# Two attention blocks on one core: layout changes through DRAM scratch, with a new planning table

## The chip, the cores and the metric

The kernel runs on one core of a Trainium2 chip. The metric is the device time of one execution in microseconds (us). A core has TensorE (PE, with its weight loads as PEld), VectorE (DVE), ScalarE (ACT), GpSimd (POOL) and SyncE (SP); in this kernel nearly all transfers are issued from SP's queue, one after the other.

## The reference

The input x is 1 x 2048 x 640. Two attention blocks with 32 heads of 20 read the same x, and a gate mixes them.

```python
x = A_x
g = sigmoid((x * gate_w).sum(-1, keepdims=True))
a = A(x, A_wqkv, A_wo)     # full softmax attention over 2048 keys
b = B(x, B_wqkv, B_wo)     # each query sees 8 keys: itself and 2, 4 .. 14 back, masked before the start
return g * a + (1 - g) * b
# A: scores = einsum("bhqd,bhkd->bhqk", q, k) * Dh**-0.5; softmax; einsum("bhqk,bhkd->bhqd"); @ wo
# B: logits over W=8 shifted copies of k (dil=2), softmax over the 8, weighted sum of 8 shifted copies of v; @ wo
```

## The kernel before, in words

**Block A.** Queries go in four chunks (`qc`) of 512 columns, heads in quads of four, so there are 32 groups `g`. A group has 64 units: 16 key blocks of 128 times 4 heads. A unit is a 128 x 512 tile of scores. TensorE writes the scores of 2 or 3 units into one of two score buffers (L1600), ACT takes the exponential of all of them in one instruction into `ebuf` (L1624), and TensorE multiplies by V into `obank` (L1669).

**The exponential on DVE.** Some units skip ACT: their scores "ride" along in a spare bank, and DVE writes an integer form of the exponential into `uD` (L1614). Four such units are a quad (`gen_d`): DVE adds three shifted copies `eD` (L863), POOL scales V (`vS`, L855), and TensorE sums four weighted products. The more quads, the less ACT has to do, and the more DVE and TensorE.

**Q's bounds.** `gen_qd` projects Q in slices of 128 features. A slice goes to `dst`, and a DMA for each piece of a head moves it into the rows of `qT` (L730). A matmul (L750) gives an upper bound of the scores for each head and query, which lies in `qbnd` with 32 heads times 4 column parts on the partitions (L757). It must become one row of 512 in `qT` for each head: for each run of heads of one quad, four DMAs (L770), one per column part.

**Block B.** It runs in 8 units `u` of 256 tokens. `gen_bproj` projects q, k and v into `qkvB` (v's part is called `vB`), with a halo of 16 tokens that POOL copies (L896). `vB` holds 4 groups of 32 heads on the partitions. Its shifted copies go to `vR`, part of the `kvw` tensor, so that each of four partition groups `w4` has all heads at its own shift: 16 DMAs per unit (L917). `gen_b` multiplies q with shifted k (L935), sums on TensorE, finds the maximum, takes the exponential `eB` on ACT (L983), and multiplies `eB` with `vR` (L1032). The reciprocal of the sum, with the gate in it, is `rQ` (L1013, L1015): 4 column parts on the partitions. Four DMAs bring it to 32 partitions of `rB` (L1018), and three more copy these to the other groups (L1020, `spread`). `rB` scales B's result into `oB` (L1065).

**Output.** `gen_norm` transposes and normalises A's result and moves it to `oTd` by DMAs for each piece (L841). `gen_fold` projects A and B for the first three query chunks; `gen_prefold` and `gen_prefold2` do this for the last chunk, as far as they can before the last group ends, and `tail` adds the last quad of heads (L1148 to L1175).

**The order.** All instructions are put in order when the kernel is built. `_Sched.task` keeps a planned clock for each engine, with a cost for each task: for a DMA, the time to its landing, and `iss` (0.75 us unless given) for each issue on SP. Each engine then runs its list in the fixed order, with semaphore waits. Side work (`gen_qd`, `gen_bproj`, `gen_b`, `gen_fold` and so on) are Python generators; each yields a request, for instance `("pe", cost, ready)`, and `run_side` takes the first one that fits into the gap that the exponentials leave. `wanted` decides whether a unit rides, and opens a quad only if enough time of the current groups remains (`DTIME`) and DVE is planned to be idle enough (`DIDLE`, `DIDLE2`, `DWAIT`). `PLAN` is the layout table: from score tile number `s` on, it sets 18 such parameters:

```python
(SLACK, XTOL, XPRIO, XLATE, DWAIT, DIDLE, DIDLE2, DTIME, DLOW, DLATE, DVE_AHEAD, DAHEAD, BOOST, XBOOST, RFILL,
 FILL, HOLD, BOFF) = plan
```

Of the kernel before, what the change touches and what calls it, by code (L numbers as in the profile page):

```python
# [5 lines left out]
FP32 = mybir.dt.float32  # L6
# [8 lines left out]
P = 128  # L15
# [35 lines left out]
    0: ((0.29, 0.69), 0.16, 1.0, 5.5, 0.94, -1.37, 0.17, 9.99, 5.5, 6.98, 0.6, 0.62, 5.69, 5.04, 0.0, 0.62, 2, -1.5),  # L51
    5: ((0.29, 0.69), 0.01, 1.0, 6.6, 1.12, -1.6, 0.17, 11.8, 2.0, 7.54, 0.6, 0.62, 4.85, 4.42, 0.0, 0.65, 2, -3),
    15: ((0.32, 0.64), 0.16, 1.0, 2.5, 0.94, -1.41, -0.97, 11.8, 7.0, 8.62, 0.62, 0.47, 4.4, 4.29, 0.0, 0.54, 2, -3),
    20: ((0.29, 0.69), 0.16, 1.0, 2.5, 0.94, -1.41, -0.97, 11.8, 7.0, 8.62, 0.62, 0.62, 5.69, 5.04, 0.0, 0.54, 2, -3),
    30: ((0.3, 0.63), 0.25, 1.0, 2.5, 1.39, -1.06, -0.43, 7.4, 7.0, 8.84, 0.7, 0.51, 4.4, 4.81, -0.2, 0.69, 1, -3),
    35: ((0.32, 0.68), 0.31, 2.5, 5.5, 0.76, -1.58, -0.5, 11.8, 7.0, 6.64, 0.35, 0.39, 4.4, 4.35, 0.0, 0.66, 2, -3),
    40: ((0.34, 0.69), 0.01, 1.0, 5.5, 0.94, -1.37, 0.17, 9.99, 7.0, 7.54, 0.6, 0.62, 5.69, 5.04, 0.0, 0.65, 2, -3),
    45: ((0.26, 0.66), 0.39, 1.0, 2.5, 0.49, -1.34, -0.97, 7.4, 7.0, 8.25, 0.52, 0.47, 4.4, 4.0, 0.0, 0.71, 3, 0.0),
    50: ((0.26, 0.75), 0.39, 1.0, 2.5, 0.49, -1.34, -0.97, 7.4, 7.0, 8.25, 0.52, 0.47, 4.4, 4.0, 0.0, 0.71, 3, 0.0),
    60: ((0.26, 0.75), 0.39, 1.0, 2.5, 0.49, -1.34, -0.97, 6.5, 7.0, 8.25, 0.43, 0.47, 4.4, 4.0, 0.0, 0.71, 3, 0),  # L60
    70: ((0.26, 0.75), 0.39, 1.0, 2.5, 0.81, -1.34, -0.97, 6.5, 7.0, 8.25, 0.43, 0.47, 4.4, 4.0, 0.0, 0.71, 0, 0),
    75: ((0.25, 0.75), 0.39, 1.0, 2.5, 0.81, -1.34, -0.97, 6.61, 7.0, 8.25, 0.43, 0.47, 4.4, 4.0, 0.0, 0.71, 0, 0),
# [12 lines left out]
    155: ((0.23, 0.7), 0.16, 1.0, 2.5, 0.94, -1.37, 0.49, 7.4, 5.5, 7.54, 0.45, 0.67, 5.69, 5.04, 0.0, 0.54, 1, -3),
    180: ((0.23, 0.7), 0.16, 1.0, 2.5, 0.94, -1.37, 0.49, 7.4, 5.5, 7.54, 0.45, 0.67, 5.69, 5.04, 0.0, 0.54, 1, 1),
    185: ((0.23, 0.7), 0.16, 5.5, 2.5, 0.94, -1.37, 0.49, 7.4, 5.5, 7.54, 0.45, 0.67, 5.69, 5.04, 0.0, 0.54, 1, -3),
    190: ((0.23, 0.7), 0.28, 5.5, 1.0, 0.94, -1.6, -0.5, 7.4, 5.5, 7.54, 0.52, 0.67, 4.64, 5.04, 0.0, 0.54, 1, -1.5),
    200: ((0.32, 0.64), 0.35, 5.5, 1.0, 0.94, -1.6, -0.5, 11.8, 7.0, 7.54, 0.52, 0.67, 4.4, 5.04, 0.0, 0.54, 1, -1.5),
    210: ((0.33, 0.64), 0.35, 5.5, 1.0, 1.02, -1.6, -0.5, 11.8, 7.0, 7.54, 0.52, 0.67, 4.4, 5.04, 0.0, 0.54, 1, -1.5),  # L80
    215: ((0.31, 0.76), 0.28, 2.5, 1.0, 0.72, -1.6, -0.65, 9.86, 7.0, 7.05, 0.52, 0.55, 5.68, 3.17, 0.0, 0.64, 2, -6),
    220: ((0.34, 0.68), 0.38, 2.5, 1.0, 0.94, -1.06, 0.05, 7.4, 7.0, 10.69, 0.6, 0.55, 3.3, 5.42, 0.0, 0.61, 1, -1.5),
    225: ((0.34, 0.68), 0.38, 2.5, 1.0, 0.82, -1.06, -0.35, 9.79, 7.0, 10.69, 0.61, 0.44, 4.4, 5.42, 0.0, 0.61, 1, 1),
    245: ((0.34, 0.68), 0.38, 2.5, 1.0, 0.82, -1.06, -0.35, 6.21, 7.0, 10.69, 0.61, 0.44, 4.4, 5.42, 0.0, 0.53, 1, 1),
    250: ((0.44, 0.72), 0.28, 2.5, 1.0, 1.21, -1.6, -0.5, 9.86, 7.0, 6.01, 0.45, 0.54, 6.04, 3.66, 0.0, 0.87, 0, -6),
    255: ((0.34, 0.68), 0.38, 2.5, 1.0, 0.94, -1.06, 0.05, 7.4, 7.0, 10.69, 0.6, 0.55, 3.3, 5.42, 0.0, 0.61, 1, -1.5),
# [293 lines left out]
def _build(ctx, nc, A_x, A_wqkv, A_wo, B_wqkv, B_wo, gate_w, out):  # L380
# [1482 lines left out]
```

## Time and profile before

| What | us |
|---|---|
| median of 3 runs (lowest, highest) | 810.18 (809.9, 811.21) |
| the profiled execution, and its span | 810.18, 808.3 |
| ACT: exponentials L1624, 707 instructions | 767.2 busy |
| DVE: L1614 (376 instructions), L863 (282) | 247.3 and 200.2 busy |
| DVE: B's products L935 and L1032, 40 each | 48.6 and 47.9 busy |
| PE: scores L1600, 2048 matmuls | 278.5 busy |

The span is the time from the first to the last instruction; 1.9 us lie around it. Busy time of an engine is the time in which at least one of its instructions ran, so the times of groups that overlap in the pipeline can't be added exactly. Lines such as L917 are lines of the kernel before. SPq is SP's queue: its rows show how long the issue of a DMA took, not how long the data moved.

### The profile page before, as it was taken

The page shows a single profiled execution, that of the slowest core. Times are in us where ns is not written, and L with a number is a line of the kernel's source. Part 1 is how long each engine was busy: PE and PEld are TensorE (multiplying, and loading weights), DVE is VectorE, ACT ScalarE, POOL GpSimd, SP SyncE. Part 2 cuts the span into 40 slices and gives each one's busy share as a digit, 9 for nine tenths or more (in the row PEclk, how much of TensorE's full clock was granted, in tenths as well). Part 3 has the DMA queues.
Part 4 walks back from the last instruction along what each step waited for, and adds up shares of the span by engine and source line. Part 5 has one row for each costly group of instructions (what it writes and reads, how often), then busy time and mean ns, then how long its engine had stood idle before and what let it go on. Part 6 is the DMA issues. An engine that isn't in the chain of part 4 may idle for free.

```text
span 808.3 us, 28593 instructions
## 1 busy us (share of the span) xinstructions
PE 749.0 (93%) x12063; PEld 285.9 (35%) x12065; DVE 721.9 (89%) x1236; ACT 779.0 (96%) x739; POOL 129.3 (16%) x193
## 2 busy tenths in 40 slices
PE   8999999999899898999999898999899899999987
PEld 5432222333233332333334323432334343234323
DVE  7587996589999999999999999899999999998865
ACT  4999999999999999999999999999999999999994
POOL 6011011011121110212112111121111212111010
PEclk9999999999999999999999999999999999999999
DMA  9112112300013131110013101313010310300221
GB/s 310 45 28 44 43 29 47 76 13 20 5 39 73 34 69 34 21 25 6 22 37 70 24 18 30 77 22 68 7 39 26 71 23 18 74 7 23 51 55 37
DMA packets 61458, 35.50 MB, mean 44 GB/s; under 512 B 27220, under 2 KB 60132, under 8 KB 61332
## 3 DMA queue, kind: packets, MB, share of 16 engines
q1 hardware_dynamic: 61044, 33.36, 17.0%
q8 instruction: 96, 1.57, 0.8%
q10 hardware_dynamic: 288, 0.33, 0.1%
q14 instruction: 30, 0.25, 0.1%
HBM read 12.00 MB, written 2.62 MB: 18 GB/s over the span
## 4 chain that ended last, share of the span: by engine, by line
PE 34%; DVE 32%; ACT 20%; issue 11%; SPq 1%; DMA 1%; POOL 0%; DVEq 0%; ACTq 0%; POOLq 0%
ACT ebuf L1624 20%; DVE uD L1614 12%; PE score L1600 10%; DVE eD L863 9%; PE side L623 9%; PE obank L1669 9%; PE score L623 3%; DVE kvw L935 3%; DVE kvw L1032 2%; DVE qkvB L909 2%; SPq L917 1%; PE obank L1690 1%; PE score L1315 1%; PE obank L523 1%; PE side L1042 1%
## 5 line engine op out<-in xcount | busy, mean ns | idle before, releaser
L1624 ACT ACTIVATE ebuf<-score 128x1024 bf16<-128x1024 f32 (+1 forms) x707 | 767.2, 1233 | 8.6 <-PE score L1600 7.4
L1600 PE MATMUL score<-qT,kT 32*128 32x512 bf16 x2048 | 278.5, 385 | 32.5 <-ACT ebuf L1624 19.5
L1614 DVE TENSOR_SCALAR uD<-score 128x512 int16<-128x512 f32 x376 | 247.3, 677 | 12.3 <-PE score L1600 11.9
L863 DVE TENSOR_SCALAR eD<-uD 128x2048 int16<-128x2048 int16 x282 | 200.2, 731 | 1.7 <-PE obank L1669 0.6
L1669 PE MATMUL obank<-ebuf,vA 128*21 128x512 bf16 x1672 | 155.7, 387 | 4.8 <-DVE oTt L824 1.3
L1600 PEld LDWEIGHTS score<-qT,kT 32*128 32x128 bf16 x2048 | 69.6, 91 | 255.7 <-ACT ebuf L1624 177.7
L855 POOL TENSOR_TENSOR vS<-vA,vw 128x252 bf16<-128x252 bf16 x94 | 70.0, 748 | 317.5 <-PE obank L1669 261.5
L1669 PE MATMUL obank<-eD,vS 128*21 128x512 bf16 x1128 | 99.4, 382 | 0.0
L623 PE MATMUL side<-xT,wBs 128*32 128x256 bf16 x2400 | 96.5, 282 | 2.3 <-DVE qkvB L909 1.5
L623 PEld LDWEIGHTS side<-xT,wBs 128*32 128x32 bf16 x2400 | 68.1, 142 | 33.1 <-issue 16.3
L1669 PEld LDWEIGHTS obank<-ebuf,vA 128*21 128x21 bf16 x1672 | 36.8, 89 | 88.0 <-issue 60.4
L830 POOL TENSOR_TENSOR rcp<-rcp,gA 128x16 f32<-128x16 f32 x31 | 8.3, 268 | 292.2 <-DVE rcp L828 292.2
L935 DVE TENSOR_TENSOR kvw<-qkvB 128x2048 bf16<-128x2048 bf16 x40 | 48.6, 1233 | 0.0
L1032 DVE TENSOR_TENSOR kvw<-kvw,eB 128x2048 bf16<-128x2048 bf16 x40 | 47.9, 1213 | 0.5 <-DMA kvw<-qkvB 0.5
L909 DVE CAST qkvB<-side 128x512 bf16<-128x512 f32 (+1 forms) x72 | 41.6, 587 | 5.1 <-PE side L623 4.9
L1669 PE MATMUL obank<-uD,vA 128*21 128x512 bf16 x376 | 36.8, 382 | 0.1
L1669 PEld LDWEIGHTS obank<-eD,vS 128*21 128x21 bf16 x1128 | 27.9, 92 | 17.1 <-issue 1.0
L836 POOL TENSOR_TENSOR oN<-oTt,rcp 128x512 bf16<-128x512 f32 x31 | 32.7, 1053 | 2.4
L824 DVE STREAM_TRANSPOSE oTt<-obank 128x512 f32<-128x512 f32 x32 | 22.6, 706 | 4.3 <-PE obank L1669 4.3
L623 PE MATMUL side<-woBp,oB 128*32 128x512 bf16 (+1 forms) x500 | 25.4, 304 | 0.9 <-DVE outsb L1193 0.5
L623 PE MATMUL side<-woA_d,oTd 128*32 128x512 bf16 (+1 forms) x496 | 25.5, 303 | 0.0
L623 PE MATMUL side<-xT,kvw 128*32 128x512 bf16 x310 | 24.3, 382 | 0.9 <-DVE qkvB L660 0.3
(180 smaller groups left out, 517.4 us busy)
## 6 DMA issues: line engine op xcount, KB each, us to landing
kvw<-qkvB SPq DMA_DIRECT2D x128, 80.6 KB
WqP<-in_A_wqkv_dram SPq DMA_DIRECT2D x16, 160.0 KB
wBs<-in_B_wqkv_dram SPq DMA_DIRECT2D x1, 2400.0 KB
oTd<-oN SPq DMA_DIRECT2D x108, 20.0 KB
qT<-dst SPq DMA_DIRECT2D x104, 20.0 KB
out_dram<-outsb SPq DMA_DIRECT2D x12, 160.0 KB
kvw<-in_A_wqkv_dram SPq DMA_DIRECT2D x2, 800.0 KB
oTd<-in_A_x_dram SPq DMA_DIRECT2D x2, 640.0 KB
```

The costliest lines, as they stand in the source:

```text
L623: ins = e.matmul(o[j:k, :], l(j) if callable(l) else l[:, j:k], r, start=(first and i == 0), stop=(last and i == n - 1), skip_group_check= ...
L824: T("dve", 0.625, lambda e: e.transpose(oTt[:, :], obank[:, :]), reads=["obank"], writes=["oTt"])
L836: T(en, c2, lambda e: e.tensor_tensor(oo, ii, ib, ALU.mult), reads=["rcp", "oTt"], writes=["oN0"])
L855: T("pool", 0.607, lambda e: e.tensor_tensor(vS[:, d % 2, :, :], _ap(vA, (kb * NQ + q) * 4 * DV, [[0, K - 1], [1, 4 * DV]]), _ap(vw, 0, [[ ...
L863: T("dve", 0.065 + 0.1334 * n, lambda e, k=k, sl=sl: e.tensor_scalar(eD[:, sl % NS, 0:512 * n].bitcast(I16), uD[d % 2][:, 0:512 * n].bitca ...
L909: t = TB(dvc(n * TOK), lambda e, o=o, i=i: e.tensor_copy(o, i), reads=[("side", b)], writes=[key])
L935: TB(dvc(CH, 2), lambda e: e.tensor_tensor(o, i0, i1, ALU.mult), reads=["qB", "kB"], writes=[("prod", i)] + (["WkA", "WvA", ("WkP", 0)] if ...
L1032: TB(dvc(CH, 2), lambda e: e.tensor_tensor(o, i0, i1, ALU.mult), reads=["eB"] + [("vR", w4) for w4 in range(4)], writes=[("prod", i)], por ...
L1600: ins = e.matmul(o, kT[32 * j:32 * j + 32, q, kb * P:(kb + 1) * P], qT[g % NQT][32 * j:32 * j + 32, :], start=True, stop=True)
L1614: t = T("dve", 0.598, lambda e: e.tensor_scalar(uD[d % 2][:, 512 * i:512 * (i + 1)].bitcast(I16), side[x], UOFF, 0.0, op0=ALU.add, op1=ALU ...
L1624: exps[s] = T("act", actc(512 * n), lambda e: e.activation(ebuf[s % NE][:, 0:512 * n], score[s % 2][:, 0:512 * n], ACTF.Exp, scale=LN2 / S ...
L1669: ins = e.matmul(obank[32 * j:32 * j + DV, :], v, src, start=(kb == 0), stop=(last and k >= len(lst) - 4), skip_group_check=True)
```

## The change

Three scratch tensors in DRAM are added. `qbnd`, `vB` and `rQ` are each written to DRAM by one DMA, whose destination pattern already orders the data by head; DMAs that read DRAM then bring them to `qT`, `vR` and `rB` with one DMA for each run of heads, one for each of four shifts, and one in all. New yields hold such a DMA back, in the planned order, until the planned time at which its source is ready. The planned landing times of two other DMAs are changed (0.5 to 0.74 and 0.72 per issue), and a condition is added to `wanted`. The table `PLAN` is replaced as a whole (102 entries before, 97 after); a few entries are shown.

```diff
 PLAN = {
-    0: ((0.29, 0.69), 0.16, 1.0, 5.5, 0.94, -1.37, 0.17, 9.99, 5.5, 6.98, 0.6, 0.62, 5.69, 5.04, 0.0, 0.62, 2, -1.5),
...
-    595: ((0.29, 0.69), 0.07, 2.5, 2.5, 1.39, -1.2, 0.05, 5.48, 2.0, 8.84, 0.54, 0.55, 5.43, 4.07, 0.0, 0.69, 2, -3),
...
-    605: ((0.29, 0.69), 0.07, 2.5, 2.5, 1.39, -1.2, -0.85, 3.41, 2.0, 8.84, 0.54, 0.55, 3.61, 4.07, 0.0, 0.54, 2, -3),
-    610: ((0.31, 0.7), 0.33, 2.5, 1.0, 0.82, -1.6, -0.34, 11.8, 7.0, 6.64, 0.61, 0.44, 4.4, 4.12, 0.0, 0.63, 2, 0),
...
-    680: ((0.51, 0.45), 0.22, 6.3, 6.6, 0.84, -1.35, -0.88, 11.3, 6.2, 7.19, 0.58, 0.46, 7.14, 4.87, -0.22, 0.65, 1, 1),
-    700: ((0.34, 0.68), 0.38, 2.5, 1.0, 0.94, -1.06, 0.05, 7.4, 7.0, 8.96, 0.6, 0.55, 3.3, 5.42, 0.0, 0.61, 1, -1.5),
+    0: ((0.3, 0.64), 0.31, 1.0, 2.5, 0.49, -1.34, -0.1, 11.8, 7.0, 6.03, 0.52, 0.47, 4.4, 4.0, 0.0, 0.71, 3, -1.5),
...
+    595: ((0.34, 0.51), 0.25, 1.0, 5.5, 0.85, -0.83, -0.43, 13.15, 2.0, 7.41, 0.7, 0.51, 8.13, 4.76, 0.12, 0.67, 1, -3),
...
+    605: ((0.34, 0.45), 0.25, 1.0, 5.5, 0.7, -0.83, -0.22, 14.41, 2.0, 7.41, 0.64, 0.51, 8.13, 4.76, 0.12, 0.67, 1, -3),
...
+    630: ((0.34, 0.45), 0.25, 1.0, 5.5, 0.7, -0.83, -0.22, 13.81, 2.0, 7.41, 0.64, 0.51, 8.23, 4.76, -0.2, 0.63, 3, -3),
+    635: ((0.32, 0.68), 0.35, 1.0, 2.5, 1.39, -1.06, 0.05, 6.74, 7.0, 8.84, 0.7, 0.47, 5.68, 4.81, 0.0, 0.69, 1, -3),
...
+    675: ((0.41, 0.45), 0.22, 6.3, 6.6, 0.84, -1.35, -0.88, 11.3, 6.2, 7.19, 0.58, 0.46, 6.92, 4.87, -0.22, 0.65, 1, 1),
+    695: ((0.46, 0.45), 0.22, 6.3, 6.6, 0.84, -1.35, -0.88, 11.3, 6.2, 7.19, 0.58, 0.46, 6.92, 4.87, -0.22, 0.65, 1, 0),
 }
@@ _build
+    qD = nc.dram_tensor("scr_q", [2 * P * P], BF16)
+    rD = nc.dram_tensor("scr_r", [TOK * 32], FP32)
+    vD = nc.dram_tensor("scr_v", [P * CN * (TOK + PADB)], BF16)
+    dap = lambda t, off, dims: bass.AP(tensor=t, offset=off, ap=[list(d) for d in dims])
@@ gen_qd
-                T("sp", 2.0 + 0.5 * len(pc), lambda e, i=i, pc=pc, qc=qc: [e.dma_start(
+                T("sp", 2.0 + 0.74 * len(pc), lambda e, i=i, pc=pc, qc=qc: [e.dma_start(
...
-                T("sp", 2.0 + 0.5 * 4 * len(runs), lambda e, runs=runs, qc=qc: [e.dma_start(
-                    _ap(qT[POS[qc, h // 4] % NQT], 0, [[1, 512]])[32 * (h % 4):32 * (h % 4 + m - 1) + 1:32, j * P:(j + 1) * P],
-                    qbnd[32 * j + lead(h):32 * j + lead(h) + m, :]) for h, m in runs for j in range(4)], reads=["qbnd"] + [("qTz", g % NQT) for g in gs], writes=[("qTb", g % NQT, f) for g in bg],
-                  dma=True, nd=4 * len(runs))
+                qs = qn[0] % 2
+                qn[0] += 1
+                yield ("pe", 0.0, sch.ready("qbnd", to="sp") - 0.2)
+                T("sp", 2.1, lambda e, qs=qs: e.dma_start(dap(qD, qs * P * P, [[P, P], [1, P]]), qbnd[:, :]),
+                  reads=["qbnd"], writes=[("qD", qs)], dma=True, iss=0.65)
+                yield ("pe", 0.0, sch.ready(("qD", qs), to="sp") - 0.2)
+                T("sp", 2.0 + 0.65 * len(runs), lambda e, runs=runs, qc=qc, qs=qs: [e.dma_start(
+                    _ap(qT[POS[qc, h // 4] % NQT], 0, [[1, 512]])[32 * (h % 4):32 * (h % 4 + m - 1) + 1:32, :],
+                    dap(qD, qs * P * P + lead(h) * P, [[P, m], [32 * P, 4], [1, P]])) for h, m in runs],
+                  reads=[("qD", qs)] + [("qTz", g % NQT) for g in gs], writes=[("qTb", g % NQT, f) for g in bg],
+                  dma=True, nd=len(runs), iss=0.65)
@@ gen_norm
-            T("sp", 2.0 + 0.5 * len(pc), lambda e: [e.dma_start(
+            T("sp", 2.0 + 0.72 * len(pc), lambda e: [e.dma_start(
@@ gen_bproj
+        VP = TOK + PADB
+        yield ("pe", 0.0, sch.ready("vB", to="sp") - 0.2)
+        T("sp", 2.9, lambda e: e.dma_start(dap(vD, 0, [[CN * VP, 4], [4 * CN * VP, 32], [1, CN * VP]]), vB[:, :, :]),
+          reads=["vB"], writes=["vD"], dma=True, iss=0.65)
         while not (done.get(("bp", u - 1)) if u else done.get(("v", KBN - 1, 1))):
             yield ("cond",)
-        for w4 in range(4):
-            lo = PADB - DIL - 2 * DIL * w4
-            T("sp", 2.0 + 0.65 * 4, lambda e, w4=w4, lo=lo: [e.dma_start(
-                vR[32 * w4:32 * w4 + 32, a * CN:(a + 1) * CN, :], vB[32 * a:32 * a + 32, :, lo:lo + VW]) for a in range(4)],
-              reads=["vB"], writes=[("vR", w4)] + (["WkA", "WvA", ("WkP", 0)] if u == 0 else []), dma=True, nd=4, iss=0.65)
+        yield ("pe", 0.0, sch.ready("vD", to="sp") - 0.2)
+        T("sp", 5.5, lambda e: [e.dma_start(
+            vR[32 * w4:32 * w4 + 32, :, :], dap(vD, PADB - DIL - 2 * DIL * w4, [[4 * CN * VP, 32], [VP, 4 * CN], [1, VW]])) for w4 in range(4)],
+          reads=["vD"], writes=[("vR", w4) for w4 in range(4)] + (["WkA", "WvA", ("WkP", 0)] if u == 0 else []), dma=True, nd=4, iss=0.65)
@@ gen_b
-        T("sp", 2.0 + 0.5 * 4, lambda e: [e.dma_start(rB[0:32, j * TQ:(j + 1) * TQ], rQ[32 * j:32 * j + 32, :]) for j in range(4)],
-          reads=["rQ"], writes=["rB"], dma=True, nd=4)
-        spread = lambda: T("sp", 2.0 + 0.5 * 3, lambda e: [e.dma_start(rB[32 * i:32 * i + 32, :], rB[0:32, :]) for i in range(1, 4)],
-                           reads=["rB"], writes=["rB"], dma=True, nd=3)
+        yield ("pe", 0.0, sch.ready("rQ", to="sp") - 0.2)
+        T("sp", 2.1, lambda e: e.dma_start(dap(rD, 0, [[TQ, 4], [TOK, 32], [1, TQ]]), rQ[:, :]),
+          reads=["rQ"], writes=["rD"], dma=True, iss=0.65)
+        spread = lambda: T("sp", 2.4, lambda e: e.dma_start(rB[:, :], dap(rD, 0, [[0, 4], [TOK, 32], [1, TOK]])),
+                           reads=["rD"], writes=["rB"], dma=True, iss=0.65)
+        yield ("pe", 0.0, sch.ready("rD", to="sp") - 0.2)
@@ wanted
-                if done.get(("q", g)) and t_end >= now + DTIME:
+                if done.get(("q", g)) and t_end >= now + DTIME and (not dquads or dquads[-1][0] <= g):
```

## The prediction, on record before the run

> **What bounds the kernel now.** I read the page first: busy time by engine, and the 40 slices.
>
> ```profile
> span 808.3 us, 28593 instructions
> PE 749.0 (93%) x12063; PEld 285.9 (35%) x12065; DVE 721.9 (89%) x1236; ACT 779.0 (96%) x739; POOL 129.3 (16%) x193
> DVE  7587996589999999999999999899999999998865
> ACT  4999999999999999999999999999999999999994
> ```
>
> ScalarE (ACT) is full in all but the first and last slice. The busy time by stretches puts numbers on it:
>
> ```profile
> 25.00:200.00 175.00, 168.97 (x2519) 58.77 (x2507) 140.33 (x265) 174.17 (x163) 20.43 (x30) 1.00 0.16 36
> 200.00:775.00 575.00, 530.69 (x8756) 203.09 (x8758) 546.42 (x903) 571.09 (x543) 96.31 (x143) 1.00 0.16 37
> 775.00:808.30 33.30, 27.37 (x562) 11.53 (x554) 17.73 (x27) 21.63 (x22) 0.32 (x1) 0.96 0.09 28
> ```
>
> After the stretch stand busy PE, PEld, DVE, ACT. From 25 to 775 us ACT is idle for 0.8 + 3.9 = 4.7 us of 750. DVE is idle for 34.7 + 28.6 = 63.3 us. So nothing between 25 and 775 can shorten the kernel unless ACT gets fewer exponentials, which means that DVE takes more of them, or unless the two ends shrink.
>
> The change works on the SP queue. Its four edited transfers, by source line (count, then least/median/most ns of one issue):
>
> ```profile
> L770 SPq DMA_DIRECT2D qT<-qbnd x168: 478/541/1452, 65.7 to 690.0; - x168
> L1018 SPq DMA_DIRECT2D rB<-rQ x32: 550/590/1598, 239.2 to 783.2; - x32
> L1020 SPq DMA_DIRECT2D rB<-rB x24: 507/590/1753, 259.6 to 787.0; - x24
> L917 SPq DMA_DIRECT2D kvw<-qkvB x128: 585/603/1683, 242.7 to 769.6; - x128
> ```
>
> That is 168 x 0.541 + 56 x 0.590 + 128 x 0.603 = 201 us of issuing. Who pays for it? All that DVE waits for any transfer, from the table of waits:
>
> ```profile
> DVE oB L1065 <- DMA rB<-rB: 1.3, 1, 1.3
> DVE qkvB L890 <- DMA kT<-qkvB: 1.2, 1, 1.2
> DVE kvw L1032 <- DMA kvw<-qkvB: 0.5, 1, 0.5
> ```
>
> Of these 1.3 + 0.5 = 1.8 us belong to edited transfers; the same table has no wait of ACT for a transfer, and one of POOL (qkvB L896, 6.4 us in two waits), an engine that is 16% busy. So the queue is busy, but its time is hidden.
>
> Last, the end of the chain of waits (start, us):
>
> ```profile
> 794.39 1.56 ACT ebuf L1624
> 795.95 0.04 issue
> 795.99 0.61 PE obank L1669 x8
> 796.60 2.23 PE score L623 x160
> 798.83 2.16 PE side L623 x40
> 800.99 2.16 PE score L623 x40
> 803.15 0.22 PE score L1148 x16
> ```
>
> After the last exponential TensorE still does 6.55 us of output projection (`gen_prefold`, its third part, and `gen_prefold2`), because B's last unit is late: its last `oB` is written at 795.05. The final normalisation on DVE ends at 799.15 (the `oN` transpose starts at 798.70, 0.45 us), so at most 803.15 - 799.15 = 4.0 us of this can go.
>
> **Part 1, the issues.** Removed are 352 DMAs, 201 us. Added are 20 writes and 42 reads for Q's bounds (168 / 4 runs = 42, in 20 batches), 8 x (1 + 4) for V, 8 x (1 + 1) for the reciprocals: 118. An issue with one end in DRAM took between 0.364 us (L1175, a row per partition) and 0.631 us (L582, a DRAM side of three dimensions): 43 to 74 us, and I take 0.6, 71 us. SP is freed of 130 us. On the path this is worth only what someone waited for: at most 1.8 us, and below nothing if a new wait is longer. The 5 us that the queue saves per batch of bounds is covered by the head start of Q: score matmuls (L1600) have no wait for a transfer in the table. If that cover went, each batch would cost its write, about 2 us, since the reads cannot be issued before the write has landed. Queued behind that wait on SP are WqP's next slice, `oTd` and `out`; `oTd` is read only when a whole query chunk is folded.
>
> **Part 2, the reciprocals.** Before, in the last unit, `rQ` ends at 781.24, four issues and a landing pass, three more issues and a landing, and `oB` starts at 788.81: 7.6 us. After it is an issue (0.6) and a landing twice. The only landing that the trace prints is 1.9 us (`out_dram<-kvw`, ACT queue, 160 KB); 2 x 2.5 = 5.0 us at the low end. At the high end the broadcast of 128 KB runs at the 96 GB/s shown below: 1.4 us more, 6.4. It saves 1.2 to 2.6 us, of which the wait of `oB` was 1.3. I take 1.3 us, on the path since it sits in the late last unit; 0 to 1.3 as bounds.
>
> **Part 3, V's shifts.** Before: 16 issues of 11.4 us (the median unit) and a landing, some 13.4 us from `vB` to `vR`. After: one write of 128 x 2720 B = 348 KB, and four reads of 330 KB that wait for it. What the write costs depends on how many DMA engines it uses. The nearest row is `woBp` (L582, 160 KB, also with a DRAM side whose first dimension is 4), issued at 220.87 us with nothing else beside it from about 223.4 to 225.1; the DMA view of 222 to 230 us, slices of 0.2 us:
>
> ```profile
> DMA  0230201522222246993000200031004010003001
> GB/s 0 38 19 0 13 13 58 172 77 102 96 96 96 100 99 131 262 270 74 5 0 0 46 16 0 0 82 21 0 0 92 10 41 0 0 20 82 0 0 36
> ```
>
> It ran at 0.2 to 0.25 of the 16 engines and 96 to 102 GB/s, while plain stores of the output reach some 350 GB/s (page: DMA 0.96 to 1.04 and 335 to 356 GB/s from 805.5 to 807). So the write takes 1.5 (landing of 1.9 less its own 160 KB at 350 GB/s) + 348 / 96 = 5.1 us, or 1.5 + 1.0 = 2.5 us if it spreads over all; I take 5.1. The reads move 1.32 MB in rows of 516 B; the same rows moved at 129 GB/s at a share of 0.54 from 760 to 772 us, so about 239 GB/s when not held up by issuing: 5.5 + 1.5 = 7.0 us. With the first issue 0.6 + 5.1 + 7.0 = 12.7 us, against 13.4 before: no gain in latency to speak of, though the diff's planner allows for 2.9 + 5.5 = 8.4. Cost on the path: nothing where `vR` is early, which the times of L917's last issue and of the first L1032 show for five of eight units (8 to 44 us apart). The other three are the second rival. The POOL wait for `vB` (6.4 us) goes, and what is next late there is nothing that ACT waits for.
>
> The Trainium skill has a rule that speaks against this part: "DMA: Bandwidth & Descriptors", in "Why a DMA increments its semaphore by 16 and not by 1", has the number of engines set by the first dimension of both sides, so that a first dimension of 4 keeps a DMA on at most 4 of 16 engines. `woBp`'s 0.2 to 0.25 agrees. Without the rule one would take 2.5 us for the write, and the V path would be 2.6 us shorter than before and not equal to it; the sum below has no term from it either way.
>
> **Part 4, the new table.** It replaces all 102 entries by 97, so every placement moves. What it can win is set by exponentials moved to DVE: 376 units of 512 columns are taken over by DVE now (94 quads), ACT does 2048 - 376 = 1672 in 767.2 us (L1624), 0.459 us each. A quad more takes 4 x 0.459 = 1.8 us from ACT and costs DVE 4 x 0.60 + 3 x 0.60 = 4.2 us (pairs of L1614 and of L863 take 1.20 us on the chain). All 63.3 idle us of DVE would hold 15 quads, but before 200 us TensorE is busy for 169.0 of 175, and the rest is scattered. I take a seventh, 9 us, or 2 quads: 3.6 us. Bounds: 5 quads more (9 us) and 3 fewer (5.4 us lost), an estimate from how the rides per 25 us vary between like stretches (8 to 17 instructions of L1614 between 200 and 775 us). At the end, entries from 595 to 630 raise the time that must remain before a quad may open (field DTIME) from between 3.4 and 11.8 to between 13.2 and 14.4. This leaves DVE to B's last units and may pull the late 6.55 us under the exponentials: 0 to 4.0 us, I take 1.0.
>
> **The sum.** The profiled execution took 810.18 us, which is also the median of the three runs (span 808.3, 1.9 around it). 810.18 - 1.3 - 3.6 - 1.0 = 804.3 us. A measurement can tell about 0.2% here (1.6 us; the runs lie between 809.9 and 811.21).
>
> **Rivals.**
> First, no change: the table finds the same number of quads, and 1.3 us of waits alone go: 808.6 to 811.8. For it: ACT has only 4.7 us of idle to give. Against it: a table that is wholly new hits the same count by chance only.
>
> Second, slower, by V's path: DVE's first product (L1032) waits for `vR`. It runs a fixed order, so `uD`, `eD` and the bank releases queue behind it. In three units (first L1032 at 446.30, 518.84, 647.80) the product came 3.8, 1.6 and 2.6 us after the last issue. If the new order puts it where the planner thinks `vR` lands, it is 12.7 - 8.4 = 4.3 us early. ACT has two score buffers, a tile of 1.1 to 1.5 us each, so it loses about 2 to 3 us each time: 6 to 9 us with three units, 816 to 819, and up to 20 us with all eight. It decides the sign once ACT loses more than the 5.9 us that the forecast gains. With the low price of the write, 2.5 us, the product would be only 1.7 us early, which ACT's buffers cover, and this rival falls. The Trainium skill's rule of part 3 is the one that would make this rival happen; the trace has the rule at work in `woBp`, but not on a transfer that DVE waits for. Against it: one wait of 0.5 us is all that this path shows now, although one unit's issue took 16.8 us.
>
> Third, slower, by fewer quads: the table gives DVE's time to B and loses 3 quads: 810.2 + 5.4 - 1.3 = 814.3. For it: the stricter DTIME at the end. Against it: that comes late, where rides already fell to 8 per 25 us.
>
> Fourth, that the edit doesn't shorten the queue: the count of 352 against 118 leaves no room for it, so it gets no chance of its own.
>
> **How the numbers follow.** Forecast (faster by over 0.2%) 0.54; no change 0.10; V's path 0.20; fewer quads 0.16. So 0.54 / 0.10 / 0.36. The forecast's own range is 797 (5 quads 9.0 + 4.0 at the end, 797.2) to 808.5. The whole range has to take in most of the two slower rivals: 797 to 818, with about 1 in 20 below and 1 in 8 above.
>
> **What would show it.** Right: L1614's count rises by about 8 and L1624's busy time falls by 3 to 4 us; the issue counts are 62, 40 and 16; the stretch from the last L1624 to the end, 12.4 us now, is about 1 us shorter or more. V's write at a DMA share near 0.25 confirms part 3. Wrong: fewer uD instructions; DVE idle before L1032 put down to a transfer; ACT idle between 25 and 775 us well over 4.7 us; or issues of the DRAM transfers far above 0.6 us, which would make SP as busy as before.

## The result, and the profile after

The changed kernel takes **830.35 us** (median of four runs, 829.89 to 832.45). The kernel before, run beside it, takes 810.04 (809.3 to 811.21). The ratio is 1.026, with a 95% interval of 1.0244 to 1.0275: slower by 20 us. The prediction said 804.3, and 797 to 818 as its range. What happened is its second rival, V's path, at more than twice the price that it gave.

The page of the changed kernel, the rows that answer to those of before:

```profile
span 828.5 us, 28420 instructions
DVE  7588896689999989987699999859999989999793
ACT  4999999999999999999699999959999999999894
```

ACT has nearly the same work as before (busy for 780.2 us, 779.0 before), but its row now has three dents, a 6, a 5 and an 8, in slices 20, 27 and 38. A slice is 828.5 / 40 = 20.7 us long, so these begin at some 393, 538 and 766 us. DVE has a 6 and a 5 in the first two as well. The middle stretch says the same in us (columns as in the prediction):

```profile
200.00:775.00 575.00, 525.15 (x8707) 201.38 (x8703) 527.06 (x878) 555.71 (x524) 94.72 (x138) 0.99 0.20 41
```

From 25 to 200 us nothing changed (ACT idle 0.9 us, 0.8 before). From 200 to 775 us ACT is idle for 575 - 555.7 = 19.3 us; it was 3.9. The table of waits names what both engines stood for (total, times, longest):

```profile
ACT ebuf L1637 <- PE score L1613: 26.0, 21, 7.4
PEld side L622 <- DVE qkvB L917: 21.0, 23, 7.4
DVE kvw L1045 <- DMA kvw<-scr_v: 16.3, 3, 6.8
```

L1045 is B's product with the shifted V (L1032 before). It waits for V's reads from DRAM three times, 16.3 us in all; it was 0.5. ACT's wait for scores grew from 7.4 to 26.0 us. That is 18.6 us, and the exponentials' busy time grew by 2.1 (769.3 against 767.2): 20.7 us, against 20.2 of span. The rest of the kernel gave nothing back.

The DMA issues did what the diff says; V's two lines (count, then least/median/most ns):

```profile
L923 SPq DMA_DIRECT2D scr_v<-qkvB x8: 558/589/600, 210.9 to 766.2; - x8
L928 SPq DMA_DIRECT2D kvw<-scr_v x32: 593/631/852, 218.4 to 776.1; - x32
```

With Q's 20 x 0.416 (L774) and 42 x 0.582 (L777) and the reciprocals' 8 x 0.580 and 8 x 0.578 the 118 issues take 66.9 us, in place of 201. The counts are the 62, 40 and 16 of the prediction.

**One of the three waits, followed through.** The timeline at 385 to 408 us (start, length, engine, line, then in brackets the idle time before it and its releaser), by engine: SP, DVE, PE, ACT.

```profile
385.17 0.57 SPq L923 DMA_DIRECT2D scr_v<-qkvB  x1
393.13 2.84 SPq L928 DMA_DIRECT2D kvw<-scr_v  x4
...
403.88 1.23 DVE L1045 TENSOR_TENSOR kvw<-kvw,eB 128x2048 bf16<-128x2048 bf16 x1 [5.64 <-DMA kvw<-scr_v]
...
405.76 0.65 PE L622 MATMUL side<-xT,wBs 128*32 128x256 bf16 x8 [5.42 <-DVE qkvB L917]
...
383.79 17.62 ACT L1637 ACTIVATE ebuf<-score 128x1536 bf16<-128x1536 f32 x17
407.11 1.02 ACT L1637 ACTIVATE ebuf<-score 128x1024 bf16<-128x1024 f32 x1 [5.70 <-PE score L1613]
```

The write is issued at 385.17; the reads wait for it and are issued at 393.13, 8.0 us later (7.5 to 8.1 in all eight units). They land when DVE's product starts, at 403.88, 10.7 us after that. DVE stands from 403.88 - 5.64 = 398.24. Behind the product in DVE's fixed order is a cast of the projection of B (L917), which frees a bank, the memory into which TensorE writes its results. TensorE, also in a fixed order, stands at the matmuls that need the bank (L622), with the next scores queued behind them. ACT finishes what is in its two buffers at 383.79 + 17.62 = 401.41 and then stands too.

The two buffers let ACT run on for 401.41 - 398.24 = 3.2 us. But at the restart the same buffers are empty: product, cast, projection and scores come first, and ACT starts 407.11 - 403.88 = 3.2 us after DVE. What was covered at the front is paid at the back, and ACT loses 5.70 us for a wait of 5.64. The other two waits read 6.84 (at 545.42) and 3.85 us (783.67) on DVE, and 7.38 and 3.21 us on ACT. In the other five units the write is as slow, but DVE's order asks for the product only after the data are in.

The end is as before. The chain after the last exponentials, where its late projection begins and where the last quad's follows it:

```profile
816.43 0.61 PE obank L1682 x8
...
822.99 1.26 PE score L1161 x29
```

From 816.43 to 822.99 TensorE still does 6.56 us of late output projection; it was 6.55.

### The profile page after: what moved, and what is told of

Read it like the earlier page. It is cut to its first block, busy times and chain, and to the rows that moved or that the text cites. A ratio compares the mean times of both kernels' runs of the same rounds, so it can differ in the third digit from the quotient of the medians.

```text
span 828.5 us, 28420 instructions
## 1 busy us (share of the span) xinstructions
PE 755.4 (91%) x12110; PEld 287.0 (35%) x12110; DVE 718.1 (87%) x1235; ACT 780.2 (94%) x734; POOL 130.5 (16%) x193
## 4 chain that ended last, share of the span: by engine, by line
DVE 27%; PE 26%; ACT 26%; issue 13%; DMA 6%; SPq 1%; POOL 0%; ACTq 0%; DVEq 0%
ACT ebuf L1637 25%; DVE uD L1627 9%; DVE eD L871 8%; PE score L1613 7%; PE side L622 7%; PE obank L1682 6%; DMA scr_v<-qkvB 3%; DMA kvw<-scr_v 3%; DVE kvw L1045 2%; PE score L622 2%; DVE qkvB L917 2%; DVE kvw L946 1%; DVE oB L1078 1%; DVE oTt L832 1%; SPq L928 1%
## 5 line engine op out<-in xcount | busy, mean ns | idle before, releaser
L1637 ACT ACTIVATE ebuf<-score 128x1024 bf16<-128x1024 f32 (+1 forms) x702 | 769.3, 1257 | 27.8 <-PE score L1613 26.0
L871 DVE TENSOR_SCALAR eD<-uD 128x2048 int16<-128x2048 int16 x282 | 198.0, 724 | 1.9 <-PE obank L1682 0.9
L863 POOL TENSOR_TENSOR vS<-vA,vw 128x252 bf16<-128x252 bf16 x94 | 72.2, 771 | 345.3 <-PE obank L1682 298.1
L622 PE MATMUL side<-xT,wBs 128*32 128x256 bf16 x2400 | 96.2, 285 | 15.5 <-DVE qkvB L917 13.5
L622 PEld LDWEIGHTS side<-xT,wBs 128*32 128x32 bf16 x2400 | 68.2, 142 | 46.2 <-DVE qkvB L917 19.6
L1045 DVE TENSOR_TENSOR kvw<-kvw,eB 128x2048 bf16<-128x2048 bf16 x40 | 48.1, 1211 | 16.3 <-DMA kvw<-scr_v 16.3
L917 DVE CAST qkvB<-side 128x512 bf16<-128x512 f32 (+1 forms) x72 | 41.7, 587 | 4.1 <-PE side L622 4.1
L1682 PEld LDWEIGHTS obank<-eD,vS 128*21 128x21 bf16 x1125 | 27.8, 92 | 16.3 <-issue 1.3
L622 PE MATMUL side<-woBp,oB 128*32 128x128 bf16 (+1 forms) x580 | 27.4, 293 | 0.4 <-DVE outsb L1214 0.3
L622 PE MATMUL side<-woA_d,oTd 128*32 128x128 bf16 (+1 forms) x560 | 27.1, 294 | 0.0
L622 PE MATMUL side<-xT,WqP 128*32 128x512 bf16 x340 | 25.6, 382 | 0.3 <-DVE outsb L1214 0.2
```

The costliest lines, as they stand in the source:

```text
L622: ins = e.matmul(o[j:k, :], l(j) if callable(l) else l[:, j:k], r, start=(first and i == 0), stop=(last and i == n - 1), skip_group_check= ...
L863: T("pool", 0.607, lambda e: e.tensor_tensor(vS[:, d % 2, :, :], _ap(vA, (kb * NQ + q) * 4 * DV, [[0, K - 1], [1, 4 * DV]]), _ap(vw, 0, [[ ...
L871: T("dve", 0.065 + 0.1334 * n, lambda e, k=k, sl=sl: e.tensor_scalar(eD[:, sl % NS, 0:512 * n].bitcast(I16), uD[d % 2][:, 0:512 * n].bitca ...
L917: t = TB(dvc(n * TOK), lambda e, o=o, i=i: e.tensor_copy(o, i), reads=[("side", b)], writes=[key])
L1045: TB(dvc(CH, 2), lambda e: e.tensor_tensor(o, i0, i1, ALU.mult), reads=["eB"] + [("vR", w4) for w4 in range(4)], writes=[("prod", i)], por ...
L1637: exps[s] = T("act", actc(512 * n), lambda e: e.activation(ebuf[s % NE][:, 0:512 * n], score[s % 2][:, 0:512 * n], ACTF.Exp, scale=LN2 / S ...
```

## The experiments

The theory after the result: V's landing is the whole loss, because the order is built for a landing of 2.9 + 5.5 = 8.4 us and the transfers take 17.5 to 18.7 from issue to use. The rivals: the new order itself is worse (fewer exponentials on DVE, or other waits), or the detour through DRAM costs time in all three places. Under the theory there was a second question, why the transfers are slow: A1, the write uses few DMA engines, since its first dimension is 4; R1, the rows of 516 B are short; R2, each read goes to 32 partitions only. Ratios below are to the kernel before, run beside each.

**V's data taken away (e1).** From the second unit on, the same DMAs in the same order carry almost nothing.

```diff
-    dap(vD, 0, [[CN * VP, 4], [4 * CN * VP, 32], [1, CN * VP]]), vB[:, :, :])
+    ... if u == 0 else dap(vD, 0, [[CN * VP, 16], [1, CN * VP]]), vB[0:16, :, :])
-    vR[32 * w4:32 * w4 + 32, :, :], dap(vD, ..., [[4 * CN * VP, 32], [VP, 4 * CN], [1, VW]])
+    ... if u == 0 else vR[32 * w4:32 * w4 + 32, 0:1, :], dap(vD, ..., [[4 * CN * VP, 32], [VP, 1], [1, VW]])
```

> The kernel after, its instruction order unchanged; from the second unit on V's write moves only 16 of 128 partitions and each read only one of 20 rows per partition, so V's data are left out and vR lands early. Theory A (V's path through DRAM lands about 9 us later than the planner allows, DVE stands 5.6 + 6.8 + 3.9 = 16.3 us in front of L1045, ACT starves for about as long): the three waits vanish, the time falls by 14 to 18 us to 812 to 816. Theory B (the new order is slower by itself and the waits only collect idle time that would come anyway): under 5 us come back, 825 or more. Theory C (the edited transfers of Q's bounds and of the reciprocals cost the time): no change, about 830.

Measured: 810.27, ratio 1.0015 (1.0002 to 1.0027). The waits and the middle stretch of e1:

```profile
ACT ebuf L1639 <- PE score L1615: 7.2, 14, 2.0
200.00:775.00 575.00, 534.58 (x8891) 204.59 (x8884) 541.75 (x900) 570.73 (x540) 96.91 (x139) 1.00 0.11 25
```

DVE has no wait for V left, and ACT's wait is that of before. The time is below the 812 to 816 that was expected: all of the 20 us come back. So V's landing is the whole loss, and the rest of the change, table and all, is worth no gain: 0.0 to 0.3% slower than before. The same windows show a wait's whole effect, 398 to 412 us of the changed kernel and of e1 (busy PE, PEld, DVE, ACT, POOL, then clock, DMA share, GB/s):

```profile
398.00:412.00 14.00, 8.47 (x118) 3.09 (x114) 7.15 (x12) 7.43 (x8) 0.80 (x2) 0.76 0.49 87
```

```profile
398.00:412.00 14.00, 12.88 (x234) 5.90 (x230) 14.00 (x23) 14.00 (x15) 0.97 (x2) 1.00 0.15 33
```

ACT loses 14.00 - 7.43 = 6.6 us there, and 8.5 around the second wait (5.55 busy of the 14 us from 541, 14.00 in e1); together they are the 15.0 us between 555.71 and 570.73. Around the third it loses 4.5 (9.46 of the 14 us from 777, 14.00 in e1). The three make 19.6 us, which is the whole difference of the spans (828.5 and 808.9). The granted clock in the first row is the other finding; it comes at the end.

**V's write on 16 engines (e2).**

```diff
-    T("sp", 2.9, lambda e: e.dma_start(dap(vD, 0, [[CN * VP, 4], [4 * CN * VP, 32], [1, CN * VP]]), vB[:, :, :]),
+    T("sp", 2.9, lambda e: [e.dma_start(dap(vD, a * CN * VP, [[4 * CN * VP, 32], [1, CN * VP]]), vB[32 * a:32 * a + 32, :, :]) for a in range(4)],
```

> The kernel after, order unchanged; V's write is cut into four DMAs of 32 partitions, whose DRAM side has 32 as first dimension, so that each can use 16 DMA engines instead of 4; layout and reads as they are. The write now lands 8.0 us after its issue. Theory A1 (the write is slow because it runs on 4 engines): it lands after 4 x 0.6 + 1.5 + 1.0 = 4.9 us, the three waits shrink by 3 us each, 821 to 823. Theory A2 (it is slow because DRAM takes it slowly or the other DMAs share the engines): still about 8 us, 829 to 832.

Measured: 817.28, ratio 1.0095 (1.0073 to 1.0116), better than expected. SP's timeline and the wait:

```profile
385.50 1.74 SPq L923 DMA_DIRECT2D scr_v<-qkvB  x4
388.64 2.91 SPq L928 DMA_DIRECT2D kvw<-scr_v  x4
...
DVE kvw L1045 <- DMA kvw<-scr_v: 6.4, 2, 3.6
```

The same bytes now land 3.1 us after the first issue in place of 8.0, although four DMAs are issued. About two thirds of the loss (1.026 - 1.0095 of 1.026 - 1.0015) was this one pattern. A1 holds.

**Long rows too (e4).** The write is one DMA with a first dimension of 128; `vR` gets the row pitch of the scratch, so that a read moves 4 runs of 2692 B per partition.

```diff
-    dap(vD, 0, [[CN * VP, 4], [4 * CN * VP, 32], [1, CN * VP]]), vB[:, :, :])
+    dap(vD, 0, [[CN * VP, P], [1, CN * VP]]), vB[:, :, :])
-    vR[32 * w4:32 * w4 + 32, :, :], dap(vD, ..., [[4 * CN * VP, 32], [VP, 4 * CN], [1, VW]])
+    vR (pitch VP)[32 * w4:32 * w4 + 32], dap(vD, ..., [[CN * VP, 32], [32 * CN * VP, 4], [1, (CN - 1) * VP + VW]])
```

> The kernel after, order unchanged, all data moved; V is written in the order of partitions (first dimension 128), and vR has a row pitch of 272, so that a read takes 4 runs of 2692 B per partition in place of 20 of 516 B. The maximum's scratch lies in rB to make room. Theory A with the landing set by engines and row length: write 3.1 us, reads 4 x 0.33 MB at some 350 GB/s and a landing 5.5 us, 8.6 us in all, what the planner allows; the waits vanish, 812 to 816, as with V's data left out. If row length does not matter: reads still 10 us, the waits shrink by 5 us each, 815 to 818. Theory B: 825 or more.

Measured: 815.11, ratio 1.0074 (1.0054 to 1.0095). The write lands in 2.2 us; one wait of 3.6 us is left, in the last unit. The interval overlaps that of e2, so the rows' own worth isn't resolved here. Nor is the wait that is left one of slow transfers alone. SP's timeline before it:

```profile
752.42 0.36 SPq L922 DMA_DIRECT2D scr_v<-qkvB  x1
755.41 4.12 SPq L848 DMA_DIRECT2D oTd<-oN  x4
759.57 1.90 SPq L927 DMA_DIRECT2D kvw<-scr_v  x4
```

In SP's fixed order four DMAs of `oTd` stand between V's write and its reads. With 2.2 us for the write, the reads could have been issued at 754.7 (an estimate); they are issued at 759.57, 4.9 us later, and DVE waits 3.6. In e2 the same four DMAs hold the last unit's reads back until 762.93, 5.9 us after the write's first issue. No run moves them out of the way.

**V by 16 copies as before, in the new order (e3).** It separates the route from the planned time: the transfers of before, with the planned 8.4 us of the change.

```diff
-    vR[32 * w4:32 * w4 + 32, :, :], dap(vD, ...)) for w4 in range(4)]
+    vR[32 * w4:32 * w4 + 32, a * CN:(a + 1) * CN, :], vB[32 * a:32 * a + 32, :, lo:lo + VW]) for w4 in range(4) for a in range(4)]
```

> The kernel after, order unchanged; V's shifts go from SBUF to SBUF in 16 copies as in the kernel before (the write to DRAM is a dummy of 16 partitions). Q's bounds and the reciprocals stay with DRAM. Theory A: dummy write 2.5, 16 issues 9.6 and a landing 2, about 14 us instead of 18; the three waits shrink by about 4 us each, 817 to 820. Theory B: 825 or more. Theory C: about 830.

Measured: 828.26, ratio 1.0236 (1.0218 to 1.0255): a miss by 8 us.

```profile
386.98 13.29 SPq L928 DMA_DIRECT2D kvw<-qkvB  x16
...
DVE kvw L1046 <- DMA kvw<-qkvB: 15.2, 3, 6.3
```

The 16 copies alone take 13.3 us to issue in this unit. In this order DVE waits nearly as long for them as for the detour (15.2 and 16.3 us). From the first issue (a small write in place of V's) to the product it is 16.2 to 19.6 us in the three units; in the longest, the last, the copies also stand behind the four DMAs of `oTd` (771.02 against 763.39). So the loss is not DRAM as such: it is a landing of 16 to 20 us in an order made for 8.4.

**The transfers by themselves (m_dma).** One kernel with nothing but the DMAs, each form waited for before the next, three rounds.

```diff
+ write 348 KB:  1 DMA, first dimension 4 | 4 DMAs x 32 | 1 DMA, first dimension 128
+ read 1.3 MB:   4 DMAs to 32 partitions, 516 B | the same, 2692 B | 1 DMA to 128 partitions, 516 B | the same, rows of 10880 B
+ 16 SBUF copies
+ broadcast of 32 KB to 128 partitions: 1 DMA, first dimension 4 | 4 DMAs x 32
```

> No attention at all: ten transfers of V and the reciprocals, each alone and waited for, three times round, with zeros for data. Writes of 348 KB: in the changed kernel's pattern (DRAM side first dimension 4), as four DMAs of 32 partitions, and as one with first dimension 128. Theory A1 (engines set by the first dimension): about 5 to 8 us for the first (8.0 in the kernel), 4 to 5 and 2.5 to 3 for the others. Theory A2 (contention in the kernel): all about 3 alone. Reads of 1.3 to 1.4 MB: four DMAs to 32 partitions each with rows of 516 B (10 us in the kernel), the same with 2692 B, one DMA to all 128 partitions with 516 B, and one with whole rows of 10880 B. Theory R1 (short rows are slow): the second and fourth are much faster than the first and third. Theory R2 (32 destination partitions at a time are slow): the first two are alike, 8 to 10 us, and the last two faster, 5 to 7. Theory R3 (DRAM reads are slow): all four alike. The 16 copies inside SBUF: issues of 0.6, 11 to 12 us. The broadcast of 128 KB with first dimension 4 against four DMAs of 32 partitions: 3.5 against 4.

Measured, in that order: 7.8, 3.1 and 2.25 us; 9.35, 8.3, 6.9 and 5.45 us; 11.9 us; 3.6 to 3.9 and 3.0 to 3.1 us. What moved, in windows inside the first and the third write and the first and the third read (columns: DVE, POOL, clock, DMA share, GB/s; the long rows reach 179 and 279 GB/s):

```profile
72.70:79.90 7.20, 0.00 (x0) 0.00 (x0) 1.00 0.18 48
83.40:85.20 1.80, 0.00 (x0) 0.00 (x0) 1.00 0.50 193
86.00:94.60 8.60, 0.00 (x0) 0.00 (x0) 1.00 0.95 154
103.60:109.80 6.20, 0.00 (x0) 0.00 (x0) 1.00 0.84 213
```

Alone on the chip the write takes 7.8 us at a share of 0.18 and 48 GB/s, so in the kernel contention adds at most 0.2 us. The reads take 9.35 us alone and 9.6 to 10.7 in the kernel. One DMA to all partitions in place of four to 32 saves 2.5 us (9.35 to 6.9), long rows save 1.0 (9.35 to 8.3) and 1.4 (6.9 to 5.45). That puts R2 before R1, with a reservation: the four DMAs all read the same 348 KB, the one reads 1.3 MB of another tensor, so the partitions are not the only difference. The broadcast came out the other way round than expected.

**Q's bounds and the reciprocals by SBUF groups, V's data away (e5).** As e1, and the two other edits' transfers go the old way, with the new planned times.

```diff
-    qT[...][32 * (h % 4):..., :], dap(qD, ..., [[P, m], [32 * P, 4], [1, P]])) for h, m in runs]
+    qT[...][32 * (h % 4):..., j * P:(j + 1) * P], qbnd[32 * j + lead(h):...]) for h, m in runs for j in range(4)]
-    rB[:, :], dap(rD, 0, [[0, 4], [TOK, 32], [1, TOK]])
+    rB[0:32, j * TQ:(j + 1) * TQ], rQ[32 * j:32 * j + 32, :] (4 DMAs), then rB[32 * i:32 * i + 32, :], rB[0:32, :] (3)
```

> As the run with V's data left out (same instruction order on every engine, V's data left out), but Q's bounds and the reciprocals go by partition groups inside SBUF again, 168 and 56 issues, with a small dummy write in place of each write of the bounds; their planned times are kept. Theory A (these two parts never were on the path): no difference from that run, 0.999 to 1.004 of the kernel before. Rival (the freed 67 us of SP issuing for these two, or the shorter chain of the reciprocals, bought something that the table used): slower than the kernel before by 0.5% or more.

Measured: 820.42, ratio 1.0127 (1.0106 to 1.0147).

```profile
DVE qbnd L771 <- DMA qT<-qbnd: 7.4, 1, 7.4
PE score L1628 <- DMA qT<-qbnd: 2.2, 2, 1.5
```

It doesn't say what the DRAM route of these two is worth: its main loss is again one transfer later than planned. Its 12 issues at 147 us take 7.25 us, and DVE, which may not overwrite `qbnd` before they have landed, waits 7.4 us for them once. Score matmuls wait for the bounds too, 2.2 us in two waits.

**The true times in the plan (e7).** Transfers as in the change; the planned landings are those measured.

```diff
-    T("sp", 2.9, ...)   # V's write
+    T("sp", 8.0, ...)
-    T("sp", 5.5, ...)   # V's reads
+    T("sp", 10.7, ...)
```

> The kernel after with two planned durations changed, V's write from 2.9 to 8.0 and its reads from 5.5 to 10.7 us, as measured; the table is kept, so the order changes wherever the planner now waits longer for V. Theory A: DVE waits under 2 us for V in all. The planner's own last end moves from 800.0 to 818.0, since the table was not made for these durations; the kernel before and the run with V's data left out both took 8 to 10 us more than their planned ends of 800.6 and 800.0, so 826 to 829. Rival (the waits have another cause than the planned durations): waits of 10 us and more stay, 835 to 845.

Measured: 826.36, ratio 1.0208 (1.0182 to 1.0234). The waits for V are gone; the group of L871 shows what was paid instead (busy, mean ns, idle before), first in the changed kernel and then in e7:

```profile
L871 DVE TENSOR_SCALAR eD<-uD 128x2048 int16<-128x2048 int16 x282 | 198.0, 724 | 1.9 <-PE obank L1682 0.9
L871 DVE TENSOR_SCALAR eD<-uD 128x2048 int16<-128x2048 int16 x261 | 182.8, 722 | 4.5 <-PE obank L1682 3.6
```

Each quad has three `eD`: 261 / 3 = 87 quads against 94. ACT's exponentials took 780.5 - 769.3 = 11.2 us more, 1.6 us for each lost quad. With planned times that are true the same table loses nearly as much time as with false ones, as fewer quads in place of waits. That the later `vR` crowds them out of the table's choices is argued, not shown.

**The old order with fast transfers (e8).** Table and order of before; all three transfers through DRAM, V's in the form of e4, a scratch of its own for each use; SP itself waits for each write.

```diff
+    def through(e, w): w.then_inc(scr, 16); scn[0] += 16; e.wait_ge(scr, scn[0])
-    4 DMAs per run qT <- qbnd; 16 DMAs vR <- vB; 4 + 3 DMAs rB
+    through(e, qD <- qbnd), 1 DMA per run; through(e, vD <- vB), 4 DMAs vR <- vD; rD <- rQ, 4 DMAs rB <- rD
```

> The kernel before with its table, planned times and instruction order on PE, ACT, DVE and POOL; only the edited transfers go through DRAM, in their fast shapes (V's write with first dimension 128, reads of 2692 B rows, the reciprocals read by four DMAs of 32 partitions; each write is waited for on SP, each with scratch of its own). All data moved. Theory A (the transfers through DRAM are worth only what someone waited for, the loss came from planned times that were too short): 1.3 us for the reciprocals at the end and 0.5 us for V, so 0.997 to 1.000 of the kernel before. Rival (DRAM transfers cost as such, by memory traffic or by SP standing about 2 us at each of 36 writes): above 1.005.

Measured: 807.68 (11 runs; before 808.92 in 15), ratio 0.9981 (0.9972 to 0.999). It is 1.2 us faster than the kernel before. SP's own waits for the two writes:

```profile
SPq L785 <- DMA scr_q<-qbnd: 32.8, 20, 4.0
SPq L933 <- DMA scr_v<-qkvB: 21.3, 8, 4.2
```

In the table of waits DVE's 1.8 us for the edited transfers are gone, and SP stands for 54 us at the two writes while ACT waits for scores no longer than before (6.1 us, 7.4 before). So in the old order the DRAM route gains no more than the 1.8 us of waits that it takes away. (To make room for V's long rows, the maximum's scratch lies in `rB` here, as in e4 and e9.)

**The change with fast transfers and a table found again (e9).** V's forms of e4, planned 2.6 and 10.0 us, and a table searched anew for these; its planned end was 802.9.

```diff
-    T("sp", 2.9, ...); T("sp", 5.5, ...); PLAN = {...}   # 97 entries
+    T("sp", 2.6, ...); T("sp", 10.0, ...); PLAN = {...}  # found anew
```

> The kernel after with the fast shapes of V's transfers, planned durations of 2.6 (write) and 10.0 us (reads), and a table searched again for these; it comes to a planned end of 802.9 (the tables of before and after: 800.6 and 800.0 with their own planned durations). Theory A (waits vanish once the planned durations hold): no wait of DVE for V above 1 us, and about 9 us over the planned end, as the kernel before and the run with V's data left out: 811 to 814. Rival (the waits stay whatever is planned): 816 or more.

Measured: 816.03 (813.24 to 818.73), ratio 1.0084 (1.0053 to 1.0115): two of the four runs lie where expected, two 5 us above. The waits for V are gone.

```profile
L919 DVE TENSOR_SCALAR eD<-uD 128x2048 int16<-128x2048 int16 x273 | 192.7, 727 | 3.0 <-PE obank L1731 2.1
```

Two slices of 2 us of the same run (busy PE, PEld, DVE, ACT, POOL, then granted clock, DMA share, GB/s):

```profile
784.00:786.00 2.00, 1.69 (x14) 0.38 (x14) 2.00 (x4) 1.75 (x2) 0.00 (x0) 0.53 0.07 21
786.00:788.00 2.00, 2.00 (x17) 0.49 (x18) 1.57 (x4) 1.47 (x2) 0.00 (x0) 0.50 0.04 10
```

Its group of `eD` counts 273 instructions, 91 quads, three fewer than before, and the exponentials take 773.8 us, 5 more than in e4 (768.8). The two groups of runs differ in TensorE's granted clock: its mean is 0.988 in both runs above 818 us and 0.997 in both near 813. The profiled run is one of those above 818. In it the clock is at 0.50 from about 784 to 794 us, though TensorE had no gap above 0.65 us in the 5 us before, and ACT waits for scores meanwhile (1.47 of 2.00 busy in the second row). Why the clock falls in some runs and not in others, and whether a longer search would reach 808, stays open.

## Why the prediction was wrong

**The step that failed is the end of part 3**: it put V's path at nothing in the sum, and the path cost all of the 20 us (e1). What happened is the second rival's mechanism: DVE's first product waits for `vR` in three units, and what is queued behind it starves ACT. The prediction's own figures had the contradiction in them: 12.7 us of transfer in an order made for 8.4. It weighed this by how early `vR` came in five of eight units of the *old* order, and gave it 0.20. A new order has no reason to keep that slack; e3 shows that in it DVE waits 15.2 us even for the transfers of before. That the rival's upper end, "up to 20 us with all eight" units, meets the measured loss is luck: it was three units, at some 6.5 us each.

**The write's price (part 3) failed by its row.** `woBp`'s 96 GB/s gave 5.1 us; it took 8.0, and 7.8 alone. `woBp` reads DRAM with a pattern of first dimension 4; V's write to such a pattern ran at 48 to 49 GB/s, half of it, at a share of 0.18 to 0.19. The share that the prediction named as the sign came true, the rate did not. The Trainium skill's rule, in "DMA: Bandwidth & Descriptors", "Why a DMA increments its semaphore by 16 and not by 1", that the first dimension sets the number of engines, agrees in that 4 took 7.8 us and 32 and 128 took 3.1 and 2.25. Cost: 2.9 us per unit.

**The reads' price (part 3) failed by its scaling.** 129 GB/s at a share of 0.54 was scaled to 239 at full share, 7.0 us; they took 9.6 to 10.7 in the three units, and 9.35 alone at 154 GB/s and a share of 0.95. At a nearly full share these reads moved 154 GB/s, so scaling the old copies' rate by their share gave a rate that did not hold. Cost: about 3 us per unit. V's whole path is then 17.5 to 18.7 us and not 12.7, and DVE stands for 3.9 to 6.8 us.

**The cover (second rival) failed.** Two score buffers were to take half of each wait. They took nothing, as the timeline above shows, and five profiles agree. Against e1 (span 808.9, ACT's wait for scores 7.2):

| kernel | DVE's waits for the late transfer | ACT's wait more | span more |
|---|---|---|---|
| e4 | 3.6 | 3.4 | 3.4 |
| e2 | 6.4 | 8.6 | 7.8 |
| e5 | 7.4 | 9.6 | 10.2 |
| e3 | 15.2 | 18.4 | 18.6 |
| after | 16.3 | 18.8 | 19.6 |

A us of DVE's waiting costs 0.9 to 1.2 us of the kernel's span; e5's 1.4 also holds the score matmuls' own waits. At this price three waits of 4.3 us would have cost 12 to 16 us, 822 to 826; with the true landings it is 20.

**The two quads (part 4) did not come.** L871 ran 282 times in both kernels, 94 quads, and the exponentials' busy time rose by 2.1 us. The estimate took a share of DVE's idle time and nothing in the trace tied the new table to it. **The 1.0 us at the end** was 0: 6.56 against 6.55, in spite of the higher DTIME.

**Two slips that enter no sum**: without the rule of part 3, V's path would have been 0.6 + 2.5 + 7.0 = 10.1 us, 3.3 shorter than before and not 2.6; and the queue saves (168 x 0.541 - 62 x 0.6) / 20 = 2.7 us per batch of bounds by the prediction's own figures, not 5.

**Right**: 118 issues and 66.9 us (71 estimated), hidden as the wait tables said; the worth of the edited transfers themselves. The prediction put at most 1.8 us on the path, 1.3 of it the reciprocals'; e8, which has the transfers without the new order, gained 1.2.

## What to carry to other kernels

In a schedule whose engines run fixed orders, ask of every new transfer when the order *expects* it, and compare that with the slowest row of its shape. Here V's write alone was 5 us later than planned in all eight units, and three of them turned the lateness into waits, of 3.9 to 6.8 us. Such a wait costs about its full length or a little more, since a short buffer ahead of the bottleneck engine is drained at the stop and has to be filled again at the restart. Time saved on a queue that nobody waits for is worth nothing, so look first at the table of waits and price only its rows. A DRAM pattern that permutes the data for free in its outermost dimension may be the slowest way to move it: put the long dimension outermost, or split the DMA.

## What the runs showed of the hardware that was not expected

**A DVE wait slows TensorE after it is over.** Slices of 2 us of the changed kernel around the first wait (busy PE, PEld, DVE, ACT, POOL, then granted clock, DMA share, GB/s):

```profile
402.00:404.00 2.00, 0.00 (x0) 0.00 (x0) 0.12 (x1) 0.00 (x0) 0.00 (x0) 0.69 0.68 156
404.00:406.00 2.00, 0.24 (x8) 0.21 (x8) 2.00 (x3) 0.00 (x0) 0.00 (x0) 0.50 0.20 45
...
408.00:410.00 2.00, 2.00 (x31) 0.67 (x23) 0.93 (x1) 1.26 (x2) 0.14 (x1) 0.60 0.07 16
410.00:412.00 2.00, 1.95 (x33) 0.75 (x33) 1.86 (x4) 1.87 (x3) 0.66 (x2) 1.00 0.02 7
```

TensorE stops at 400.35. At about 402.8 (0.69 in the mean of 402 to 404) its granted clock falls to 0.50, and it stays there until about 409.6 (0.60 in the mean of 408 to 410), 3.8 us after work is back at 405.76: score matmuls that took 0.39 us each take 0.6 there. TensorE has no gap in 408 to 410 (2.00 busy), and ACT, waiting for its scores, is busy for 1.26 us of them, with DVE's wait long over. This is how a us of waiting can cost more than one. After the three stops of TensorE the clock fell 2.4, 2.3 and 4.2 us after its last matmul (which ended at 400.35, 540.45 and 780.85; the clock fell at about 402.76, 542.7 and 785.06). The third fall came when work was just back, at 784.95. The Trainium skill, "TensorE: Matmul & The Clock Gate", "Part 1: The HAM clock gate (the "warmup" mystery)", says that an idle window of about 3.4 us halves the clock. The halving agrees with the rows; two of the three falls came earlier than that, and in e9 the clock fell with no gap above 0.65 us in the 5 us before.

**Four DMAs to 32 partitions each are slower than one to 128**, 9.35 against 6.9 us for the same rows of 516 B, and 8.3 against 5.45 with long ones. The Trainium skill, "SBUF — State Buffer", "Door 1: The DMA port swizzle (why `[64,N]` ≈ `[32,N]`)", says that 32 partitions reach 8 of 16 ports; 154 and 179 GB/s against 213 and 279 agree in direction. The four issues, 2.8 us in all, are not what holds the four DMAs back: from 88 to 93 us the DMA share reads 1.24, and yet only 184 GB/s move. That the ports are the cause is not shown, as the source differs too.
